# Sinkhorn attention and a residual MLP on one core: part of q loaded in fp32 by SyncE and cast on ScalarE, v sorting and half of a weight permutation on GpSimd

## The chip, the cores and the metric

The kernel runs on one core of a Trainium2 chip. The core has five engines with an instruction stream each: TensorE (PE, matmuls and weight loads), VectorE (DVE), ScalarE (ACT), GpSimd (POOL) and SyncE (SP, which here only starts transfers). Sixteen DMA engines move the data. Transfers started by GpSimd run on the software queue and can change the type on the way; those started by SyncE run on a hardware queue and are loaded in the type that they have. The metric is the device time of one execution in microseconds (us); lower is better.

## What is computed

The attention first normalises a small matrix per batch and head with five Sinkhorn rounds, mixes the blocks of keys and values with it, and attends block by block. Its output goes through a residual MLP over tokens and then over channels.

```
q, k, v: (4, 8, 768, 64)   sort_net: (4, 8, 8, 8)   8 blocks of 96 rows
P = sort_net
5 times:
    P = exp(P - max(P, -1));  P = P / (sum(P, -1) + 1e-9);  P = P / (sum(P, -2) + 1e-9)
k_sorted, v_sorted = einsum('bhij,bhjcd->bhicd', P, blocks of k, of v)
scores = q_block @ k_sorted_block.T / sqrt(64);  attn = softmax(scores)
x = attn @ v_sorted_block, heads side by side                # (4, 768, 512)
a1 = alpha1 * x + beta1
tok = einsum('ts,bsd->btd', w_tok, a1);   u = x + lam * tok   # w_tok: (768, 768)
a2 = alpha2 * u + beta2
ch = max(a2 @ w_ch1, 0) @ w_ch2;  out = u + lam * ch          # w_ch1: (512, 2048), w_ch2: (2048, 512)
```

## The kernel before

The code is one stream of calls in Python; its order is the order on each engine. A small wrapper class (line 55) pins every instruction in program order, which is why nearly all rows of the profile carry line 65; groups are told apart by the names of their tiles. There is no planner: what stands earlier in the text stands earlier in its engine's queue. Two pools of accumulators exist, psA (two wide tiles, `psa`) and psB (four one-bank tiles, `psb`); tiles in SBUF share slots by tag, and a tile that takes a slot over waits until the last reader of the earlier one is done.

The four batches are worked one after another. Batch 0 is special: its operands are loaded and prepared at the start, in an order written out by hand, and this stretch, about the first 36 us, is what the change edits. From then on the matmuls of the MLP of one batch (`h_unit`, `ch_unit`, `ch_pair`) run with the attention of the next put between them, through a table of slots (`put`, `run`).

The stretch in question goes as follows.

- Loads. SP loads P (sort_net), then six small vectors (lines 99 to 108). POOL loads q, k and v of batch 0 with a cast to f16: two transfers of two slabs each for q and k (`load_slabs`), two halves for v (`load_halves`), then w_tok in four pieces (tiles wt), the broadcast vectors alphaB, betaB and lamB, W1p in four parts, W2p in four parts, and later raw v, raw k and qn of batch 1. Between these issues POOL builds the identity (ident), clears padding and copies.
- Sinkhorn rounds (the loop `for it in range(5)`). Each round is one exp on ACT and six small operations on DVE, the last of which writes P again (P16 in the fifth round). After the DVE part of a round come `mask(it)` (small masks msk, mhi, mth, mgap made from the identity) and what the table `beside` lists for it: `q_first(g)` turns slab g of q on PE (q_ps), `q_out(g)` copies it on ACT into qT, `prep_ab2` turns the small vectors, and `warm(n)` fills PE with n matmuls of zeros (warm_ps).
- Mixing. `mix_keys` replicates P16 on PE (repk_ps) and makes the block matrix bigK on DVE (selk, redk, bigK); `mix_values` makes bigV. `k_turn(0, g)` multiplies a slab of k by bigK (k_ps), and `k_copy` brings it to kT on DVE or ACT.
- Values. `v_sort(lo, hi, engine)` copies columns lo to hi of v8 into VD with the last two axes exchanged (vd<-v): in this kernel columns 16 to 32 and 48 to 64 on POOL, 0 to 8 and 8 to 16 on ACT, 32 to 48 on DVE. `v_mix(0, n)` multiplies columns 8n to 8n+8 by bigV (v_ps) into Vs, with one filler matmul in every second call. The gap column of Vs is filled from mgap on DVE.
- Scores and values. `score(0, g, hf, pool)` makes eight matmuls (sc_ps) into a wide tile and one exp of 128 or 96 by 768 on ACT (et). `pv_first(g)` multiplies et by Vs (24 matmuls, x_ps); DVE then takes the reciprocal (rc) and multiplies (x).
- Token weights. `permute(half, engine, lo, hi)` reorders the columns of one half of w_tok (wp<-wt), `wtok(ks)` turns it on PE (wtok_ps) into w_tokT; `row_sum(m)` sums rows of w_tok on ACT (a<-wt, with an accumulator read), `row_sums` turns the three sums into a row (rr_ps, rrow).
- First MLP products. `first_mm(g)` (tok_ps), `first_turn(g)` (turn_ps, with brow = beta1 * lam on POOL), z and tok on ACT, a2T on DVE; then h_ps, the first large product.

Of the kernel before, what the change touches and what calls it, by code (L numbers as in the profile page):

```python
# [16 lines left out]
def kernel(  # L17
# [20 lines left out]
    nc = tc.nc  # L38
# [60 lines left out]
    nc.sync.dma_start(P32[:], sort_net.rearrange("b h i j -> (b h) i j"))  # L99
    ab2 = att.tile([4 * CT, 128], FT, name="ab2", tag="sel", bufs=2)  # L100
# [16 lines left out]
    def load_slabs(dst, src):  # L117
        flat = src[0].rearrange("h s d -> (h s d)").rearrange("(g p f) -> p g f", p=128, f=12 * D)
        for g in range(0, H4, 2):
            pool.dma_start(dst[:, g:g + 2, :], flat[:, g:g + 2, :])  # L120
# [19 lines left out]
    load_slabs(q8, q)  # L140
# [36 lines left out]
    pool.dma_start(alphaB[:], moe_alpha1.partition_broadcast(128))  # L177
    pool.dma_start(betaB[:], moe_beta1.partition_broadcast(128))
    pool.dma_start(lamB[:], moe_lam.partition_broadcast(128))
    v_sort(16, 32, pool.tensor_copy)  # L180
    for g in range(4):
        if g == 1:
            v_sort(48, 64, pool.tensor_copy)
        pool.dma_start(W1p[:, :, g * 512:(g + 1) * 512], w1v[:, :, g * 512:(g + 1) * 512])
    pool.tensor_tensor(brow[0:1, :], bet1[:], lam1[:], ALU.mult)

# [24 lines left out]
    def mask(n):  # L211
# [3 lines left out]
        elif n == 1:  # L215
            dve.tensor_reduce(msk[:], ident16[:].rearrange("p (b j) -> p b j", j=NB), AXX, ALU.add)
            dve.tensor_tensor(mhi[:], msk[:, 0:8], msk[:, 8:16], ALU.add)
            dve.tensor_reduce(mth[:], ident16[:].rearrange("p (th c) -> p th c", th=2), AXX, ALU.add)
        elif n == 2:
# [70 lines left out]
    def q_out(g):  # L290
        for half in range(2):
            q_copy(0, g, qps[g], half, act.copy)

    beside = {
        0: [lambda: q_first(0), lambda: warm(3)],
        1: [lambda: q_first(1), lambda: warm(2), lambda: warm(3)],
        2: [lambda: q_first(2), lambda: warm(3)],
        3: [lambda: q_out(0), lambda: q_first(3)],
# [3 lines left out]
    for it in range(5):  # L302
# [12 lines left out]
        if it < 3:  # L315
# [4 lines left out]

    for g in range(4):
        pool.dma_start(W2p[:, g * 4:(g + 1) * 4, :], w2v[:, g * 4:(g + 1) * 4, :])
# [96 lines left out]
    def score(b, g, hf, ps):  # L419
        ps = ps([128, 2, 512], FT, "sc_ps")  # L420
        n = 128 if b == 0 else BLK
        keys = kT_of[b][:].rearrange("p g i t -> p (g i t)")
        for ii in range(4):
# [3 lines left out]
            for h2 in range(2):  # L427
                r = slice(h2 * 64, h2 * 64 + 64)
                pe.matmul(
                    ps[0:w, h2, ii * BLK:(ii + 1) * BLK], keys[r, lo:lo + w],  # L430
# [4 lines left out]
        act.activation(  # L435
            et[0:n].rearrange("p a i t -> p a (i t)"), ps[0:n, :, 0:4 * BLK], AF.Exp, scale=scale
        )
# [666 lines left out]
```

## Time and profile before

| what | value |
|---|---|
| median of 3 runs | 259.13 us (258.68 to 259.93) |
| profiled execution, its own time | 258.79 us |
| its span, first to last instruction | 257.0 us |
| granted TensorE clock | 1.000 |
| share of the span that the chain of waits gives to PE | 75% |
| the same for DVE, DMA, ACT, issue | 10%, 7%, 4%, 2% |
| repk_ps starts (end of the Sinkhorn rounds) | 11.79 us |
| v of batch 0 complete | 16.38 us |
| first h_ps | 35.88 us |

A row of a timeline gives the start in us, the length in us, the engine, the operation and its tiles as out<-in, how many of them the row holds, and in brackets how long the engine was idle before it and what released it. A row of the chain gives the start, the length and whose work it was; "issue" there is time in which the engine waited for nothing that the profile shows. A row of the windows view gives a stretch, its length, and for PE, weight loads (PEld), DVE, ACT and POOL the busy time and the number of instructions, then the granted clock, the DMA engines' busy share and GB/s. The digits of the slices are tenths of busy time in 40 equal parts of the span, 6.4 us each; the software and the instruction queue are shown with packets, MB and share of the sixteen engines.

### The profile page before, as it was taken

How to read it: one execution, taken by the hardware profiler on the slowest of the kernel's cores; microseconds unless marked ns; L12 is line 12 of the kernel's file. 1: busy time of each engine (PE TensorE's matmuls, PEld its weight loads, DVE VectorE, ACT ScalarE, POOL GpSimd, SP SyncE). 2: the span in 40 equal slices, each digit the busy share in tenths (PEclk: the TensorE clock that was granted, in tenths of full speed). 3: DMA queues.
4: the chain of work that ended last, by engine and by line, in shares of the span. 5: the costliest groups of instructions: out<-in, count | busy, mean ns of one | idle time of the engine just before them, and what ended most of it. 6: DMA issues, size and time to landing. Idle time of an engine off the chain costs nothing.

```text
span 257.0 us, 5959 instructions
## 1 busy us (share of the span) xinstructions
PE 246.4 (96%) x2371; PEld 159.7 (62%) x2371; DVE 176.3 (69%) x467; ACT 155.3 (60%) x282; POOL 44.2 (17%) x67
## 2 busy tenths in 40 slices
PE   7998799999999999999999999999999999999994
PEld 3465565555555545456865787557756875686783
DVE  6796888595539945759896675298887773461873
ACT  3567767485997539787565587877465004847400
POOL 8759302700074000047000000000000000000000
PEclk9999999999999999999999999999999999999999
DMA  5999999998999957999994259810202232111022
GB/s 99 214 203 179 209 205 211 214 151 173 122 209 187 150 128 159 143 136 192 145 143 120 41 135 170 151 20 3 84 0 42 62 101 65 23 40 41 3 82 82
DMA packets 67535, 31.07 MB, mean 121 GB/s; under 512 B 56674, under 2 KB 63218, under 8 KB 67508
## 3 DMA queue, kind: packets, MB, share of 16 engines
q0 software_dynamic: 26352, 15.34, 46.4%
q1 hardware_dynamic: 41060, 15.33, 33.6%
q8 instruction: 18, 0.29, 0.5%
q14 instruction: 9, 0.07, 0.1%
q10 hardware_dynamic: 96, 0.03, 0.1%
HBM read 32.79 MB, written 8.65 MB: 161 GB/s over the span
## 4 chain that ended last, share of the span: by engine, by line
PE 75%; DVE 10%; DMA 7%; ACT 4%; issue 2%; SPq 1%; DVEq 0%; POOLq 0%
PE h_ps L65 27%; PE tok_ps L65 10%; PE px L65 8%; PE pz L65 6%; PE py L65 6%; DVE x L65 5%; PE ch_ps L65 4%; PE x_ps L65 3%; DMA Vs<-vscr 3%; PE warm_ps L65 2%; DMA vscr<-mixed 2%; PE sc_ps L65 2%; DMA q<-in_q_dram 2%; DVE a L65 2%; PE v_ps L65 1%
## 5 line engine op out<-in xcount | busy, mean ns | idle before, releaser
L65 PE MATMUL h_ps<-a2T,W1p 128*128 128x384 bf16 x512 | 93.2, 326 | 0.0
L65 PEld LDWEIGHTS <-W1p 128*128 128x128 bf16 x512 | 47.9, 98 | 31.3 <-issue 0.2
L65 ACT ACTIVATE hTa<-h_ps 128x384 f16<-128x384 f32 x64 | 31.2, 493 | 27.3 <-PE h_ps L65 26.4
L65 ACT ACTIVATE hTb<-h_ps 128x384 f16<-128x384 f32 x64 | 31.2, 490 | 7.6 <-PE h_ps L65 7.6
L65 DVE SCALAR_TENSOR_TENSOR u<-tok_ps,x 128x512 f32<-128x512 f32 x21 | 14.5, 690 | 26.0 <-PE tok_ps L65 26.0
L65 PE MATMUL tok_ps<-a,w_tokT 128*128 128x512 f16 x126 | 30.3, 379 | 0.5 <-DVE a L65 0.5
L65 ACT CAST kT<-kmix_ps 64x512 f16<-64x512 f32 x36 | 25.8, 716 | 4.9 <-PE kmix_ps L65 4.4
L65 ACT ACTIVATE et<-sc_ps 96x768 f16<-96x768 f32 (+1 forms) x32 | 24.8, 808 | 3.7 <-PE sc_ps L65 3.7
L65 ACT CAST u<-u 128x512 f16<-128x512 f32 x21 | 13.0, 618 | 22.9 <-DVE u L65 22.9
L65 PEld LDWEIGHTS <-sums 128*128 128x128 f16 x216 | 21.1, 98 | 3.3 <-issue 0.2
L65 PEld LDWEIGHTS <-hTb 128*128 128x128 f16 x200 | 18.6, 98 | 6.3
L65 PEld LDWEIGHTS <-hTa 128*128 128x128 f16 x192 | 18.3, 98 | 6.4
L65 PEld LDWEIGHTS <-w_tokT 128*128 128x128 f16 x126 | 12.3, 98 | 13.8 <-issue 1.0
L65 DVE TENSOR_TENSOR x<-x_ps,rcb 96x512 f16<-96x512 f32 x24 | 16.5, 687 | 0.8
L65 POOL DMA_DIRECT2D qn<-in_q_dram x18 | 16.0, 913 | 4.3 <-DMA raw<-in_v_dram 4.2
L65 DVE TENSOR_TENSOR sums<-hTa,hTb 128x512 f16<-128x512 f16 (+2 forms) x27 | 8.9, 330 | 10.4 <-ACT hTb L65 10.0
L65 PEld LDWEIGHTS <-et 96*128 96x128 f16 (+4 forms) x288 | 11.8, 100 | 5.3 <-DVE x L65 1.6
L65 PE MATMUL x_ps<-Vs,et 96*128 96x65 f16 (+4 forms) x288 | 13.0, 195 | 1.8 <-DVE x L65 0.9
L65 DVE SCALAR_TENSOR_TENSOR ost<-px,u 128x256 f32<-128x256 f32 x27 | 11.3, 417 | 3.5 <-PE px L65 3.5
L65 PE MATMUL warm_ps<-wz 128*128 128x512 f16 x36 | 11.0, 439 | 1.2 <-DVE wz L65 1.2
L65 PE MATMUL ch_ps<-W2p,hTb 128*128 128x512 f16 x48 | 12.0, 379 | 0.0
L65 ACT CAST mixed<-mix_ps 128x1024 f16<-128x1024 f32 x9 | 9.1, 1012 | 4.7 <-PE mix_ps L65 4.5
(139 smaller groups left out, 352.9 us busy)
## 6 DMA issues: line engine op xcount, KB each, us to landing
out_dram<-ost SPq DMA_DIRECT2D x23, 192.0 KB, 2.7
raw<-in_v_dram POOLq DMA_DIRECT2D x6, 384.0 KB, 6.9
raw<-in_k_dram POOLq DMA_DIRECT2D x6, 384.0 KB, 9.5
qn<-in_q_dram POOLq DMA_DIRECT2D x18, 128.0 KB, 10.5
vscr<-mixed SPq DMA_DIRECT2D x6, 384.0 KB, 5.2
Vs<-vscr SPq DMA_DIRECT2D x3, 768.0 KB
W1p<-in_moe_w_ch_dram POOLq DMA_DIRECT2D x4, 512.0 KB, 11.9
W2p<-in_moe_w_ch_dram POOLq DMA_DIRECT2D x4, 512.0 KB, 17.4
```

Of the source, the lines that this page charges most:

```text
L65: ins = getattr(self.eng, name)(*args, **kwargs)
```

## The change

The first two slabs of q are no longer loaded by POOL with a cast. SP loads them in fp32 into a tile q32, right behind P and ahead of the small vectors, and ACT casts each with two copies, after the exps of the second and the third Sinkhorn round. The q turns and warm-ups in `beside` move accordingly, and the masks are made one per round, with mgap after bigV.

After the rounds, `k_turn(0, 0)` and its copies follow `mix_keys` directly, and `mix_values` takes its accumulator from psA. POOL makes brow, sorts columns 16 to 56 of v and fills the gap column before it issues alphaB, betaB, lamB and W1p; ACT sorts columns 0 to 8 and 56 to 64, DVE 8 to 16. The second half's permute goes from DVE to POOL, between the issues of W1p and W2p. Three of the scores go to two one-bank tiles in psB, with an exp of 384 columns each. The first half's permute is done in one go before the first `pv_first`; the row sums on ACT, `wtok(4)` (DVE to ACT), `pv_first(1)` to `pv_first(3)` and `prep_scales` change places. Nine warm-up matmuls fall away.

```diff
@@ -97,6 +97,11 @@
     dve.memset(wz[:].bitcast(FT), 0.0)
     P32 = const([BH, NB, NB], FT, "P32")
     nc.sync.dma_start(P32[:], sort_net.rearrange("b h i j -> (b h) i j"))
+    q32 = moep.tile([128, 2, 12 * D], FT, name="q32", tag="x128", bufs=1)
+    for g in range(2):
+        nc.sync.dma_start(
+            q32[:, g, :], q[0].rearrange("h s d -> (h s d)").rearrange("(g p f) -> p g f", p=128, f=12 * D)[:, g, :],
+        )
     ab2 = att.tile([4 * CT, 128], FT, name="ab2", tag="sel", bufs=2)
     nc.sync.dma_start(ab2[0:CT, :], moe_alpha2.rearrange("(c p) -> c p", p=128))
     nc.sync.dma_start(ab2[CT:2 * CT, :], moe_beta2.rearrange("(c p) -> c p", p=128))
@@ -114,9 +119,9 @@
     k8 = att.tile([128, H4, 12 * D], F16, name="k8", tag="raw", bufs=2)
     v8 = att.tile([128, HB, D], F16, name="v8", tag="raw", bufs=2)
 
-    def load_slabs(dst, src):
+    def load_slabs(dst, src, lo=0):
         flat = src[0].rearrange("h s d -> (h s d)").rearrange("(g p f) -> p g f", p=128, f=12 * D)
-        for g in range(0, H4, 2):
+        for g in range(lo, H4, 2):
             pool.dma_start(dst[:, g:g + 2, :], flat[:, g:g + 2, :])
 
     def load_halves(dst, src):
@@ -137,7 +142,7 @@
 
     brow = att.tile([128, C], F16, name="brow", tag="uT", bufs=2)
     rrow = att.tile([128, 384], F16, name="rrow", tag="uT", bufs=2)
-    load_slabs(q8, q)
+    load_slabs(q8, q, 2)
     ident16 = const([128, 128], F16, "ident16")
     pool.memset(ident16[:], 0.0)
     pool.affine_select(
@@ -174,16 +179,6 @@
     alphaB = const([128, C], F16, "alphaB")
     betaB = const([128, C], F16, "betaB")
     lamB = att.tile([128, C], FT, name="lamB", tag="kT", bufs=1)
-    pool.dma_start(alphaB[:], moe_alpha1.partition_broadcast(128))
-    pool.dma_start(betaB[:], moe_beta1.partition_broadcast(128))
-    pool.dma_start(lamB[:], moe_lam.partition_broadcast(128))
-    v_sort(16, 32, pool.tensor_copy)
-    for g in range(4):
-        if g == 1:
-            v_sort(48, 64, pool.tensor_copy)
-        pool.dma_start(W1p[:, :, g * 512:(g + 1) * 512], w1v[:, :, g * 512:(g + 1) * 512])
-    pool.tensor_tensor(brow[0:1, :], bet1[:], lam1[:], ALU.mult)
-
     vscr = dram.tile([B, H * NB, BLK, D], F16, name="vscr", tag="vscr")
     raw_of = {}
     qn_of = {}
@@ -214,9 +209,11 @@
             dve.tensor_reduce(mlo[:], ident16[:].rearrange("p (b j) -> p j b", j=NB), AXX, ALU.add)
         elif n == 1:
             dve.tensor_reduce(msk[:], ident16[:].rearrange("p (b j) -> p b j", j=NB), AXX, ALU.add)
+        elif n == 2:
             dve.tensor_tensor(mhi[:], msk[:, 0:8], msk[:, 8:16], ALU.add)
+        elif n == 3:
             dve.tensor_reduce(mth[:], ident16[:].rearrange("p (th c) -> p th c", th=2), AXX, ALU.add)
-        elif n == 2:
+        elif n == 4:
             dve.tensor_reduce(
                 mgap[:], ident16[:].rearrange("p (th t) -> p th t", th=2)[:, :, 0:HB],
                 mybir.AxisListType.XY, ALU.add,
@@ -291,11 +288,15 @@
         for half in range(2):
             q_copy(0, g, qps[g], half, act.copy)
 
+    def q_cast(g):
+        for f in (slice(0, 6 * D), slice(6 * D, 12 * D)):
+            act.copy(q8[:, g, f], q32[:, g, f])
+
     beside = {
-        0: [lambda: q_first(0), lambda: warm(3)],
-        1: [lambda: q_first(1), lambda: warm(2), lambda: warm(3)],
-        2: [lambda: q_first(2), lambda: warm(3)],
-        3: [lambda: q_out(0), lambda: q_first(3)],
+        0: [],
+        1: [lambda: q_cast(0), lambda: q_first(0), lambda: warm(3)],
+        2: [lambda: q_cast(1), lambda: q_first(1), lambda: warm(3), lambda: q_first(2)],
+        3: [lambda: q_out(0), lambda: warm(3), lambda: q_first(3)],
         4: [lambda: q_out(1), lambda: q_out(2), lambda: q_out(3), lambda: prep_ab2(psb), lambda: warm(4)],
     }
     warm(12)
@@ -312,14 +313,11 @@
             (P16 if it == 4 else P32)[:], P32[:],
             csum[:].unsqueeze(1).to_broadcast([BH, NB, NB]), ALU.mult,
         )
-        if it < 3:
+        if it < 4:
             with nc.allow_low_precision(reason="sums of zeros and a one"):
                 mask(it)
         for f in beside[it]:
             f()
-
-    for g in range(4):
-        pool.dma_start(W2p[:, g * 4:(g + 1) * 4, :], w2v[:, g * 4:(g + 1) * 4, :])
 
     bigK = {}
     bigV = {}
@@ -417,7 +415,12 @@
     kT_of = {0: KT0}
 
     def score(b, g, hf, ps):
-        ps = ps([128, 2, 512], FT, "sc_ps")
+        if ps is psb:
+            ps = [ps([128, 4 * BLK], FT, "sc_ps") for _ in range(2)]
+            bank = [t_[:] for t_ in ps]
+        else:
+            ps = [ps([128, 2, 512], FT, "sc_ps")]
+            bank = [ps[0][:, a, :] for a in range(2)]
         n = 128 if b == 0 else BLK
         keys = kT_of[b][:].rearrange("p g i t -> p (g i t)")
         for ii in range(4):
@@ -427,14 +430,20 @@
             for h2 in range(2):
                 r = slice(h2 * 64, h2 * 64 + 64)
                 pe.matmul(
-                    ps[0:w, h2, ii * BLK:(ii + 1) * BLK], keys[r, lo:lo + w],
+                    bank[h2][0:w, ii * BLK:(ii + 1) * BLK], keys[r, lo:lo + w],
                     qT_of[b][r, g, i * BLK:(i + 1) * BLK], start=True, stop=True,
                 )
         tag, bufs = ("ost", 4) if (b, g) == (0, 3) else ("et", 6)
         et = att.tile([128, 2, 4, BLK], F16, name="et", tag=tag, bufs=bufs)
-        act.activation(
-            et[0:n].rearrange("p a i t -> p a (i t)"), ps[0:n, :, 0:4 * BLK], AF.Exp, scale=scale
-        )
+        if len(ps) == 1:
+            act.activation(
+                et[0:n].rearrange("p a i t -> p a (i t)"), ps[0][0:n, :, 0:4 * BLK], AF.Exp, scale=scale
+            )
+        else:
+            for a in range(2):
+                act.activation(
+                    et[0:n, a].rearrange("p i t -> p (i t)"), ps[a][0:n, :], AF.Exp, scale=scale
+                )
         ets[(b, g, hf)] = et
 
     x_of = {}
@@ -891,15 +900,28 @@
         prep_wtok(ks, 0, psb, eng)
 
     mix_keys(0, psb)
-    warm(3)
-    mix_values(0, psb)
-    prep_scales()
-    dve.tensor_copy(Vs[:, :, D:GRP], mgap[:].unsqueeze(2).to_broadcast([128, H * NB, GRP - D]))
     kp0 = k_turn(0, 0, psb)
-    kp1 = k_turn(0, 1, psb)
     k_copy(0, 0, kp0, 0, copy)
     k_copy(0, 0, kp0, 1, act.copy)
-    warm(3)
+    mix_values(0, psa)
+    with nc.allow_low_precision(reason="sums of zeros and a one"):
+        mask(4)
+    pool.tensor_tensor(brow[0:1, :], bet1[:], lam1[:], ALU.mult)
+    v_sort(16, 32, pool.tensor_copy)
+    v_sort(32, 48, pool.tensor_copy)
+    pool.tensor_copy(Vs[:, :, D:GRP], mgap[:].unsqueeze(2).to_broadcast([128, H * NB, GRP - D]))
+    v_sort(48, 56, pool.tensor_copy)
+    pool.dma_start(alphaB[:], moe_alpha1.partition_broadcast(128))
+    pool.dma_start(betaB[:], moe_beta1.partition_broadcast(128))
+    pool.dma_start(lamB[:], moe_lam.partition_broadcast(128))
+    for g in range(4):
+        pool.dma_start(W1p[:, :, g * 512:(g + 1) * 512], w1v[:, :, g * 512:(g + 1) * 512])
+    permute(1, pool.tensor_copy, 0, 6)
+    for g in range(4):
+        pool.dma_start(W2p[:, g * 4:(g + 1) * 4, :], w2v[:, g * 4:(g + 1) * 4, :])
+    warm(1, psa)
+    kp1 = k_turn(0, 1, psb)
+    warm(1)
     kp2 = k_turn(0, 2, psb)
     k_copy(0, 1, kp1, 0, copy)
     k_copy(0, 1, kp1, 1, act.copy)
@@ -907,13 +929,13 @@
     k_copy(0, 2, kp2, 0, copy)
     k_copy(0, 2, kp2, 1, act.copy)
     v_sort(0, 8, act.copy)
-    v_sort(8, 16, act.copy)
+    v_sort(56, 64, act.copy)
     score(0, 0, 0, psa)
     k_copy(0, 3, kp3, 0, copy)
     k_copy(0, 3, kp3, 1, copy)
+    prep_scales()
     score(0, 0, 1, psa)
-    v_sort(32, 48, copy)
-    warm(2, psb)
+    v_sort(8, 16, copy)
     v_mix(0, 0, psb, copy)
     v_mix(0, 1, psb, copy)
     score(0, 1, 0, psa)
@@ -925,31 +947,29 @@
     score(0, 2, 0, psa)
     v_mix(0, 6, psb, copy)
     v_mix(0, 7, psb, act.copy)
-    score(0, 2, 1, psa)
-    row_sum(0)
     permute(0, copy, 0, 3)
+    permute(0, copy, 3, 6)
     moe_start(0)
-    warm(1, psb)
+    score(0, 2, 1, psb)
     pv_first(0)
-    score(0, 3, 0, psa)
     wtok(0, copy)
     wtok(1, act.copy)
     wtok(2, copy)
-    permute(0, copy, 3, 6)
+    row_sum(0)
+    pv_first(1)
+    score(0, 3, 0, psb)
     row_sum(1)
+    pv_first(2)
+    score(0, 3, 1, psb)
     row_sum(2)
-    pv_first(1)
     wtok(3, copy)
-    wtok(4, copy)
+    wtok(4, act.copy)
     wtok(5, copy)
-    permute(1, copy, 0, 6)
-    score(0, 3, 1, psa)
-    pv_first(2)
+    pv_first(3)
     row_sums(psb)
     first_mm(0, psb)
     first_turn(0, psb)
     first_mm(1, psb)
-    pv_first(3)
     first_turn(1, psb)
     first_mm(2, psb)
     scale_affine(alphaB)
```

## The prediction

> **What bounds the kernel now.** I read the page's busy table and its 40 slices first, to find where TensorE is idle; then the chain of waits in order of time, and the waits of PE; then the timelines of DVE, ACT and POOL over the first 36 us, the only stretch that the change touches; last the DMA queues.
>
> ```profile
> PE 246.4 (96%) x2371; PEld 159.7 (62%) x2371; DVE 176.3 (69%) x467; ACT 155.3 (60%) x282; POOL 44.2 (17%) x67
> PE   7998799999999999999999999999999999999994
> DMA  5999999998999957999994259810202232111022
> PEclk9999999999999999999999999999999999999999
> q0 software_dynamic: 26352, 15.34, 46.4%
> q8 instruction: 18, 0.29, 0.5%
> ```
> PE is busy for 246.4 of 257.0 us at full clock. Only slices 1, 4 and 5 and the tail fall under nine tenths, so a gain must come from the first 36 us, where PE is idle for about 5 us, and must then survive to the end. In those slices the DMA engines are nearly full.
>
> ```profile
> 11.86 0.20 PE repk_ps L65 x4
> 13.55 1.04 PE k_ps L65 x48
> 15.34 0.68 PE k_ps L65 x24
> 21.06 1.08 issue
> 22.14 0.47 PE v_ps L65 x19
> 27.68 0.66 issue
> 28.34 0.35 PE x_ps L65 x6
> ```
> This is the chain. It passes the five Sinkhorn rounds (P, q turns and warm-ups up to repk_ps at 11.86), the key mix, the scores and value mix, and holds two pieces of "issue", in which PE waits for no semaphore. They are odd enough to look at: they end at 22.14 and 28.34, and the windows view counts between those two times
>
> ```profile
> 22.14:28.34 6.20, 5.01 (x128) 3.85 (x128) 4.80 (x11) 5.24 (x10) 4.94 (x6) 1.00 1.18 201
> ```
> exactly 128 matmuls and 128 weight loads, 256 PE instructions in 6.20 us. Counting 256 back from 22.14 reaches about 16.15, a stretch of 6.0 us. The DMA view shows packets on the instruction queue (18 in all, 0.29 MB, so 16 KB each) at 19.7 and 25.9 us, each about 2.4 us before a stall ends. I read this as PE waiting for its next 256 instructions, which travel on DMA engines that the software queue keeps full. That fits two stalls only, so it is a reading.
>
> ```profile
> 6.03 0.26 ACT L65 ACTIVATE P<-P 32x64 f32<-32x64 f32 x1 [1.51 <-DVE P L65]
> 8.20 0.26 ACT L65 ACTIVATE P<-P 32x64 f32<-32x64 f32 x1 [1.92 <-DVE P L65]
> 6.23 0.39 DVE L65 TENSOR_TENSOR mhi<-msk 128x8 f16<-128x8 f16 x1
> 6.54 0.27 DVE L65 TENSOR_REDUCE mth<-ident 128x2 f16<-128x128 f16 x1
> 16.43 1.51 POOL L65 COPY vd<-v 128x768 f16<-128x768 f16 x1 [0.57 <-DMA v<-in_v_dram]
> 30.66 1.40 DVE L65 COPY wp<-wt 128x1728 f16<-128x1728 f16 x2
> ```
> Here the reader sees the period of the Sinkhorn rounds (exps at 2.51, 4.27, 6.03, 8.20, 9.96: 1.76 us each, but 2.17 in the third, where two masks sit in front of the row sum), POOL's copy of v waiting for v's landing at 16.38, and DVE's second permute, which holds the reciprocal behind it until 31.97 although its matmuls were done at 30.98.
>
> **The change, part by part.** The sum is made against the profiled execution: 258.79 us, a span of 257.0 and 1.8 around it. It is 0.34 under the median of 259.13, so I add 0.34 at the end.
>
> Masks, one per round: the round of 2.17 falls to 1.76, as msk alone (0.27, from 5.93) ends before the exp does (6.29). mhi (0.39) now stands in the fourth round's gap, in which mgap (0.23) left 0.16 idle: it just fits. Gain 0.41, and P16, done at 11.69, comes at 11.28. PE was itself busy until 11.86 and follows only if its own queue is shorter too, which the casts decide.
>
> q on SyncE: SP's two loads stand behind P's and in front of six small ones, which move back by about 0.8 us (two issues of 0.40). Their readers, the ab_ps turn at 10.7 and brow, have slack: the last landed about 6. POOL issues one DMA fewer (771 ns), so k, v and wt start about 0.8 earlier. The slabs are 768 KB of fp32 for 384 KB cast on the way, but SP's packets of 2048 B took 84 ns and the software queue's of 1536 B 135 ns: 384 packets are 2.0 us of 16 engines, 256 packets were 2.2. So no engine time is saved; what is won is the hole in front, since software packets run dense only from 3.5 us. P landed 1.74 after its issue (0.75 to 2.49). Slab 0, issued at 1.2, would land near 1.2+1.74+1.0 = 3.9, slab 1 a us later at about 5. v then lands 1.0 to 1.2 earlier, near 15.3.
>
> The Trainium skill, page "DMA: Bandwidth & Descriptors", section "Issuing engines are not separate DMA queues", speaks against this step: transfers from SyncE and GpSimd share the same 16 engines, and only sequencer time is saved. By the page alone v would gain only the 0.77 of POOL's issue, and by the rows 1.0 to 1.2, from the idle engines before 3.5.
>
> The casts: four on ACT, nearest row qT at 464 ns for 128x384, about 0.9 a pair. ACT idles 1.50 between exps, so both pairs are covered, if slab 0 lands by 5.1 and slab 1 by 6.9 (exp at 7.79 less 0.9). Later than that, the next exp waits behind the cast on ACT's queue, and DVE's row sum and P16 behind it. PE is tighter still. In its order the second slab's turn is followed by three warm-ups, the third turn, three warm-ups, the fourth turn, the ab_ps turn and four warm-ups: by the chain's pieces 0.49 + 0.75 + 0.49 + 0.75 + 0.49 + 0.16 + 0.97 = 4.1. If the second cast starts as the exp ends, at 6.3, it ends at 7.2 and repk_ps can start at 11.3, tied with P16. So PE loses from a landing of slab 1 after 6.3. Bounds for slab 1: 4.2 (nothing in front) and 8.5, from SP's small loads issued at 2.24 to 2.88 whose packets came at 5.0 to 6.0, 2.8 to 3.1 us later, plus its own transfer behind a full queue. I take 5, by P's row, since it is issued before POOL's data run dense.
>
> Keys, scores, warm-ups: k_turn(0) follows the key mix at once and its copies precede the value masks, so the second pair of k turns moves with P16: 0.4 to 0.6 earlier. The crossing into the next 256 instructions lies in the last k turn in both orders. Gain here -0.5, with bounds 0.3 to 0.6. The count of matmuls falls by nine; warm-ups filled waits, so I price them at nothing, covered by the fetch; without that cover they would be worth at most 9 x 0.25 (three pass in 0.75) = 2.2.
>
> 16 to 28 us: if PE waits for instructions, the 6.0 and 6.2 us stay as they are, whatever the data do: v 1.1 us earlier, a 16-column copy of 1.18 on DVE halved, the gap copy (0.23) off DVE, split exps. All these are priced at 0, covered by the 1.08 + 0.66 of stalls. Should the cover go, the split exps cost most: three of 0.81 become pairs of about 0.45, +0.1 each.
>
> The Trainium skill, page "Runtime: NRT & Kernel Launch", section "Instruction fetch mechanics", says that instructions arrive in blocks of 256 over the sequencer's own queue and that crossing a block is mostly hidden. The size agrees with the 128+128 above; "mostly hidden" does not, with 1.74 us of stalls. By that sentence the stalls would have another cause and the v part would gain up to 1.1 more.
>
> 28 to 36 us: pv_first(1) is now before the crossing, seven matmuls of 0.04 less after it: -0.3. Against it, ACT's three row sums (0.84+0.20 each) now follow the scores; the last may end near 31, so rr_ps at 31.6 instead of 30.9 and PE idle, +0.6. The second permute leaves DVE (1.40), but PE is unbroken there, so 0. I take 0, between the ends -0.3 and +0.6.
>
> POOL: brow (1.26), copies of 1.5, 1.5 and 0.76, and the gap copy (about 0.3) now all stand ahead of alphaB, betaB, lamB (issues 0.60, 0.55, 0.54) and W1p (four of 0.82): W1p issues from about 21 instead of 17.9. The permute on POOL is 2304 elements: 1.9 by DVE's 1.48 times 1513/1180 of the v copies, 4.5 by POOL's 1513 ns for 768. Then W2p goes out from 27 to 29 instead of 24.1, and raw v after it. The queue hides it: lamB, issued at 15.3, landed at 26.33, W1p's last part at 36.47, eleven us and more behind. A hole of up to 1 us may open between wt's end and alphaB. Raw v landed at 50.29 for a use at 51.99, and qn at 60.02 for 60.92, and all starts 0.8 earlier: 0, bounds 0 and +0.5. After 36 us PE is unbroken, and a gain at 36 carries.
>
> Sum: -0.5 (Sinkhorn and keys) + 0 (fetch) + 0 (28 to 36) + 0 (POOL) = 258.3 for this execution, 258.6 against the median.
>
> **The rivals.**
> Stalls go: the earlier start or a less crowded queue lets instructions come in time. Then 1.74 more is won: 258.6 - 1.74 = 256.9. For it: v, the k copies and DVE all have room. Against it: the engines stay full from 3.5 to 50 us.
>
> Slabs late (other side): slab 1 lands behind software packets. From a landing of 6.3 each us costs one, by PE's order; it eats the gain of 0.5 at 6.8, and at 8.5 costs 2.2: 258.6 + 2.2 = 260.8, slower. For it: the 2.8 to 3.1 us of SP's later loads. Against: P's 1.74.
>
> POOL's late issues: if the permute takes 4.5 and a hole of 2 us opens, raw v and qn come 1 us too late: 259.6. Against: the backlog of eleven us.
>
> The change does not do what it says: the scores and row sums on ACT give back all, 259.1.
>
> **How the numbers follow.** Forecast 0.40, stalls go 0.21, slabs late 0.21, POOL late 0.08, all given back 0.10. Half a per cent, 1.3 us, is about what a measurement tells from no change. The forecast's own range is 258.0 to 259.2 and lies within it; faster is the stalls' case and some partial loss of a stall, 0.30; slower is most of slabs late and half of POOL late, with a little unknown, 0.25; same 0.45. The range from 256.7 to 260.5 takes in the first rival and most of the second.
>
> **What would show it.** Exps every 1.76 us with casts between them show the slabs in time; an exp behind a cast that waits for q shows the rival. repk_ps near 11.4 and v landing near 15.3. PE's two issue stalls, 256 instructions apart, at about 21.6 and 27.8: there, the forecast; gone, the first rival. mix_ps or qt_ps waiting for a DMA shows POOL's. I am wrong if the stalls grow, or if row sums on ACT hold rr_ps by more than 0.6.

## The result, and the profile after

The changed kernel takes 261.62 us (median of 5 runs, 260.91 to 261.80) against 259.26 for the kernel before on the same chip: a ratio of 1.008, 95% interval 1.0055 to 1.0105. It is 2.4 us slower; I had forecast 258.6 and a range up to 260.5. The profiled execution is one of 261.65 us with a span of 259.9, 2.9 more than before's 257.0. The ratios here and below leave out executions more than 1.5% above the fastest of the same kernel, four in all.

The page of the changed kernel:

```profile
PE 246.1 (95%) x2362; PEld 159.9 (62%) x2362; DVE 176.6 (68%) x463; ACT 157.5 (61%) x290; POOL 46.3 (18%) x70
PE   8768899999999999989999999999999999999994
PEclk9997999999999999999999999999999999999999
```

PE has as much busy time as before (246.1 against 246.4), though it makes nine warm-ups fewer, and its idle time has grown from 10.6 to 13.8 us. The fourth slice now shows seven tenths of the full clock. The chain of waits says where; the columns are start, length and whose work:

```profile
1.67 5.65 DMA q<-in_q_dram
7.34 0.92 ACT q L65 x2
9.68 1.30 DVE P L65
19.36 1.21 DVE vd L65
26.43 1.36 DVE wp L65 x2
33.46 0.33 PE rr_ps L65 x3
```

The two pieces of "issue" of 1.08 and 0.66 us that the chain held before are gone: the waits of PE hold none for issue, and the two pieces of 0.55 and 0.35 that the chain still has stand in front of DVE's and ACT's work. Other waits took over. Slab 1 of q lands at 7.32 us (1.67 + 5.65); the fourth exp stands behind its cast. A product on DVE lasts 1.30. DVE's copy of v and its permutes are on the path, then ACT's row sums before rr_ps. So repk_ps starts at 12.80 instead of 11.79, the first x_ps at 26.72 instead of 24.52, the first h_ps at 37.64 instead of 35.88.

The timelines of DVE and POOL, side by side, tell more than either does:

```profile
7.50 0.21 DVE L65 TENSOR_TENSOR P<-P,csum 32x64 f32<-32x64 f32 x1
9.68 1.29 DVE L65 TENSOR_TENSOR P<-P,csum 32x64 f32<-32x64 f32 x1
18.59 0.85 DVE L65 TENSOR_TENSOR ab2col<-ab2col 128x4 f32<-128x4 f32 x2
19.36 1.20 DVE L65 COPY vd<-v 128x384 f16<-128x384 f16 x1
```

```profile
9.64 1.25 POOL L65 TENSOR_TENSOR brow<-bet,lam 1x512 f16<-1x512 f32 x1
16.27 2.92 POOL L65 COPY vd<-v 128x768 f16<-128x768 f16 x2 [5.38 <-DMA v<-in_v_dram]
19.38 0.81 POOL L65 COPY vd<-v 128x384 f16<-128x384 f16 x1
20.14 0.62 POOL L65 DMA_DIRECT2D alphaB<-in_moe_alpha_dram  x1
```

Two rows of DVE in the kernel before, for comparison:

```profile
14.42 0.35 DVE L65 TENSOR_TENSOR ab2col<-ab2col 128x4 f32<-128x4 f32 x2
17.45 1.18 DVE L65 COPY vd<-v 128x768 f16<-128x768 f16 x1
```

The product P<-P,csum takes 0.21 us where POOL makes no copy or product; at 7.50 POOL was clearing a tile (a memset, 7.02 to 7.99), and it took 0.21 all the same. In the fourth round it begins as POOL's brow runs, and ends at 10.97, just after brow (10.89). The first of the two ab2col products lasts 0.62 us, until POOL's second copy of v ends (19.19); the second takes 0.19. DVE's copy of v ends 0.4 after POOL's third (20.19). Beside POOL's copies of ebh, from 5.09 to 5.86, a sum (0.25) and a reciprocal (0.19) keep their length, and the product behind them, begun at 5.57, takes 0.37 and ends at 5.94. It is the products with two operands in SBUF, and the f16 copies within SBUF, that wait. The copy of 1.18 in the kernel before may already hold such a wait, as POOL's first copy of v ran until 17.94.

In the changed kernel the second value mix waits for DVE's copy of v, and then the clock goes. In the windows view the columns after the length are PE, PEld, DVE, ACT and POOL, the granted clock, DMA share and GB/s:

```profile
18.00:20.00 2.00, 0.75 (x21) 0.41 (x17) 1.97 (x5) 1.93 (x3) 2.00 (x3) 1.00 1.15 207
20.00:22.00 2.00, 1.39 (x47) 1.04 (x49) 1.79 (x3) 0.63 (x1) 2.00 (x5) 0.97 0.34 60
22.00:24.00 2.00, 2.00 (x51) 1.36 (x49) 0.69 (x1) 1.48 (x3) 2.00 (x3) 0.50 0.65 76
```

PE idles from 18.75 to 20.61, and from about 21.9 to 25.3 its granted clock is a half. In the same rows the DMA engines run dry: 60 GB/s from 20 to 22 us, where the kernel before has 135. POOL issues alphaB at 20.14, 10 us later than before, and nothing else is queued behind w_tok. The last part of W1p lands at 37.52 (36.47 before).

### The profile page after: what moved, and what is told of

The parts are those of the page before. It is cut to its first block, busy times and chain, and to the rows that moved or that the text cites. A ratio compares the mean times of both kernels' runs of the same rounds, so it can differ in the third digit from the quotient of the medians.

```text
span 259.9 us, 5954 instructions
## 1 busy us (share of the span) xinstructions
PE 246.1 (95%) x2362; PEld 159.9 (62%) x2362; DVE 176.6 (68%) x463; ACT 157.5 (61%) x290; POOL 46.3 (18%) x70
## 4 chain that ended last, share of the span: by engine, by line
PE 73%; DVE 10%; DMA 7%; ACT 6%; issue 1%; SPq 1%; DVEq 0%
PE h_ps L65 28%; PE tok_ps L65 10%; PE px L65 8%; PE pz L65 6%; PE py L65 5%; PE ch_ps L65 4%; DMA Vs<-vscr 3%; PE sc_ps L65 2%; DMA q<-in_q_dram 2%; DVE x L65 2%; DMA vscr<-mixed 2%; PE x_ps L65 2%; PE v_ps L65 2%; DVE a L65 1%; DVE ost L65 1%
## 5 line engine op out<-in xcount | busy, mean ns | idle before, releaser
L65 PE MATMUL tok_ps<-a,w_tokT 128*128 128x512 f16 x126 | 30.3, 379 | 0.4 <-DVE a L65 0.4
L65 ACT ACTIVATE et<-sc_ps 96x768 f16<-96x768 f32 (+2 forms) x35 | 25.1, 755 | 4.0 <-PE sc_ps L65 4.0
L65 PE MATMUL ch_ps<-W2p,hTa 128*128 128x512 f16 x48 | 11.8, 379 | 0.0
```

Source lines behind the costliest of these rows:

```text
L65: ins = getattr(self.eng, name)(*args, **kwargs)
```

## Experiments

Ratios are to the kernel before on the same chip, with 95% intervals. A kernel's times behind the median come from several executions, its timeline from one.

### Which part of the Sinkhorn stretch: brow, the slabs, or both undone

brow back behind W1p's issues:

```diff
-    pool.tensor_tensor(brow[0:1, :], ...)          # ahead of the copies of v
     for g in range(4):
         pool.dma_start(W1p[...], w1v[...])
+    pool.tensor_tensor(brow[0:1, :], bet1[:], lam1[:], ALU.mult)
     permute(1, pool.tensor_copy, 0, 6)
```

> The changed kernel with one edit: GpSimd's product brow goes back behind the four issues of W1p, out of the Sinkhorn rounds. Port theory: in the changed kernel DVE's product P<-P,csum of the fourth round, 0.21 us elsewhere, lasts 1.29 us (9.68 to 10.97) because GpSimd's brow runs from 9.64 to 10.89 and the two engines cannot both read SBUF operands; here it is 0.21 again, the fifth exp comes about 1.07 earlier, P16 at about 11.65 instead of 12.73. TensorE's own queue then sets repk_ps, at about 12.5 instead of 12.80, so the time falls by only 0.3 to 0.5, to about 261.2. Rival, something else on DVE (its instructions coming late): the 1.29 us stay, and so does the time, 261.6.

Measured 262.87 us, 1.0147 (1.0108 to 1.0186): slower, not faster. The profiled execution is one of the two slowest of six (264.57). In it the product of the fourth round took 0.21 again, as expected, but slab 1 landed at 8.32, a microsecond later still, and hid what brow gave; and POOL's permute, pushed back by brow, now met DVE's permutes, for which wtok_ps waited 2.0 us. A miss.

q by GpSimd again, casts gone:

```diff
-    q32 = ...; nc.sync.dma_start(q32[:, g, :], ...)
-    load_slabs(q8, q, 2)
+    load_slabs(q8, q)
-        1: [lambda: q_cast(0), lambda: q_first(0), lambda: warm(3)],
+        1: [lambda: q_first(0), lambda: warm(3)],        # and the same for q_cast(1)
```

> The changed kernel with q loaded by GpSimd with a cast, as before, and no casts on ScalarE; all else as changed. Late-slab theory: the fourth exp no longer waits behind the cast of slab 1 (which landed at 7.32 us) and the rounds are 1.76 us each up to the fourth; brow, one transfer issue later at about 10.4 us, then holds a product of the fifth round, so P16 comes at about 11.8 and repk_ps at about 11.9 instead of 12.80: 0.9 less, 260.7. Port theory alone: P16 stays late by one blocked product, 0.4 less at most. Rival, the slabs do not matter since v and the values set the time: 261.6 unchanged.

Measured 261.42, 1.0098 (1.0078 to 1.0117). repk_ps came at 12.10, 0.7 earlier, but the second value mix began at 20.66 as in the changed kernel (20.61): it now waited 2.2 us for DVE's copy of v instead of 1.9. The gain ended there.

Both edits together:

> Both edits: q by GpSimd and brow behind W1p's issues; what is left of the change is the order on TensorE, DVE and GpSimd from 12 us on, and the masks. If the two things are the whole loss of the Sinkhorn stretch, P16 comes at about 11.3 and repk_ps at about 11.35, 1.45 earlier than in the changed kernel, and the time is 261.6 - 1.45 = 260.2. If the loss is mostly behind 16 us (v's copy on DVE, the halved clock from 22 to 25 us, the row sums), the gain is swallowed there by waits and the time stays over 261.

Measured 263.01, 1.0162 (1.0142 to 1.0182). repk_ps starts at 11.83. PE then waits 2.1 us for DVE's copy of v and 2.3 for DVE's permutes (four copies of 4.15 us that took 1.34 before; brow and POOL's permute ran beside them), and the clock is halved twice. Being early in front did no good, since the next wait is on POOL, and what was taken out of one collision ran into another.

The port alone, on the kernel before: brow moved forward, ahead of alphaB.

```diff
+    pool.tensor_tensor(brow[0:1, :], bet1[:], lam1[:], ALU.mult)
     pool.dma_start(alphaB[:], ...)
```

> The kernel before with one edit: brow goes on GpSimd right behind the issues of w_tok, ahead of alphaB's, so that it runs from about 10.4 to 11.65 us, inside the fifth round. Port theory: DVE's product that starts while brow runs (P<-P,rsum at 10.7, 0.21 us before) lasts until brow ends, about 11.7, and P16 comes at 12.6 instead of 11.69: about 0.9 later up to k_ps, and the time is 0.5 to 0.9 longer, 259.8 to 260.2. Without a shared port: unchanged, 259.3.

The timelines of this kernel, first DVE, then POOL:

```profile
10.48 0.19 DVE L65 RECIPROCAL rsum<-rsum 32x8 f32<-32x8 f32 x1
10.71 1.03 DVE L65 TENSOR_TENSOR P<-P,rsum 32x64 f32<-32x64 f32 x1
```

```profile
10.40 1.26 POOL L65 TENSOR_TENSOR brow<-bet,lam 1x512 f16<-1x512 f32 x1
```

Beside brow the reciprocal keeps its 0.19 us, and the product takes 1.03 instead of 0.21. That DVE's product waits for POOL's is shown. repk_ps came 0.76 later (12.55). Yet the time was 259.27, 1.0018 (1.0004 to 1.0032), about 0.5 us: the two issue stalls shrank from 1.08 and 0.66 to 0.33 and 0.39, and h_ps came only 0.24 later. The stalls absorb delays, as the forecast had it, up to their size.

The rule is in the Trainium skill, page "SBUF — State Buffer", section "Who interferes with whom": a DVE instruction with two inputs in SBUF contends with a GpSimd instruction that reads SBUF, and one that uses both ports (f16 copies can) with any; whoever starts first holds the shared ports for its whole length. The rows agree in both kinds, and the last of all runs below has a copy held by a copy that began before it (1.07 us instead of 0.51). The other order occurs too: in the first run of this section DVE's copy of v and POOL's began together at 20.31, DVE's kept 0.51 us, and POOL's took 1.22 instead of 0.81. My prediction did not use this rule, and it speaks against the change in three places.

### Which part behind 16 us: v's copy, the permute, the clock

Columns 8 to 16 on ACT, 56 to 64 on DVE later, the two products back behind the value mask:

```diff
-    v_sort(56, 64, act.copy)
+    v_sort(8, 16, act.copy)
-    prep_scales()          # behind the key copies
-    v_sort(8, 16, copy)
+    v_sort(56, 64, copy)   # behind score(0, 1, 1)
     mix_values(0, psa)
+    prep_scales()
```

> The changed kernel with v's columns 8 to 16 on ScalarE again, as before, columns 56 to 64 on VectorE behind the fourth value mix, and the two small scale products (ab2col) back behind the value mask. Theory: in the changed kernel the second value mix waits 1.86 us for DVE (18.75 to 20.61), because DVE's ab2col products (0.85 for two that took 0.35) and its copy of v (1.20) stand behind GpSimd's copies of v; TensorE's idling then halves its granted clock from about 21.9 to 25.3 us. Here the second value mix waits at most 0.3, the clock stays at 1.00, the first x_ps comes about 2.5 earlier than 26.72, and the time falls by 1.5 to 2.5, to 259.1 to 260.1. Rival, the row sums on ScalarE and DVE's permutes set the end of the stretch: rr_ps stays at 33.5 and the time at 261.

Measured 261.50, 1.0086 (1.0059 to 1.0113), from 259.6 to 262.9. The wait was gone and h_ps came at 36.33, but then x_ps waited 1.1 us for Vs and qt_ps 0.2 for qn, which the kernel before did for 0.2 and not at all. The clock, expected to stay at 1.00, was halved from 15.2 to about 22 us.

The second permute on DVE again:

```diff
-    permute(1, pool.tensor_copy, 0, 6)
     wtok(5, copy)
+    permute(1, copy, 0, 6)
```

> The changed kernel with the second half's permute on VectorE again, behind its last w_tokT copy of the stretch. Port theory: GpSimd's permute (24.77 to 27.07) holds DVE's first-half permutes, four copies of 2.09 us from 26.43 that took 1.34 in the kernel before; here they take 1.34 and the first wtok_ps comes 0.6 earlier; 0.4 to 0.7 less time, 261.0. Against it: 1.40 us more work on DVE beside x. Rival, the permute on GpSimd helps as meant: the time rises to 262 or more.

Measured 261.72, 1.0097 (1.0069 to 1.0124): no change. In its profile qt_ps waited 1.3 us for qn.

Six filler matmuls in the second value mix:

```diff
-        fill(..., 1 - n % 2)
+        fill(..., 6 if (b, n) == (0, 1) else 1 - n % 2)
```

> The changed kernel with six filler matmuls of zeros in the second value mix, into its own accumulator, where TensorE waited 1.86 us for DVE; nothing else. Clock theory: the wait itself stays (v_ps again at about 20.6), but TensorE counts as busy, the granted clock stays at 1.00 from 21 to 26 us, that stretch is 1.5 us shorter, and the time falls by 1.0 to 1.5, to 260.4. Rival, the low clock costs nothing since the stretch waits for others: unchanged at 261.6.

Measured 261.42, 1.0081 (1.0049 to 1.0112). The profiled execution is inconclusive: in it the clock was halved from 17.1 us on already, before the fillers, which themselves ran at half rate (six in 2.74 us). But two of the seven executions had a mean clock of 1.00 and took 261.66 and 263.38, so a full clock alone does not bring the time back.

All four undone: the diffs above for q, the columns and the permute, and brow behind W2p's issues:

```diff
-    pool.tensor_tensor(brow[0:1, :], ...)      # ahead of the copies of v
         pool.dma_start(W2p[...], w2v[...])
+    pool.tensor_tensor(brow[0:1, :], bet1[:], lam1[:], ALU.mult)
```

> All of it undone at once: q by GpSimd, brow behind W2p's issues, columns 8 to 16 on ScalarE, the second permute on VectorE. What is left of the change: one mask per round, the order of the key turns and of row sums and scores, v's other columns on GpSimd ahead of W1p, split exps, fewer warm-ups. If the four are the whole loss, no wait on DVE or ACT over 0.6 us is left before 28 us, the clock is 1.00, h_ps starts at 35.9 or earlier and the time is 258.0 to 259.3, the kernel before or better. If the order left over costs too (row sums last, W1p late), it is 260 or more.

Measured 261.73, 1.0093 (1.0075 to 1.0112). The first of its views is the timeline of PE, the second has rows of the waits of PE from 40 to 120 us (us in total, times, longest):

```profile
21.61 0.37 PE L65 MATMUL v_ps<-bigV,vd 64*64 64x64 f16 x11 [0.41 <-issue]
27.81 0.93 PE L65 MATMUL x_ps<-Vs,et 128*128 128x65 f16 x21 [0.99 <-issue]
35.45 0.74 PE L65 MATMUL h_ps<-a2T,W1p 128*128 128x384 bf16 x3
```

```profile
PE qt_ps L65 <- DMA qn<-in_q_dram: 1.7, 2, 1.4
PE x_ps L65 <- DMA Vs<-vscr: 0.8, 1, 0.8
PE mix_ps L65 <- DMA raw<-in_v_dram: 0.4, 1, 0.4
```

Now the stretch is as I had forecast it: repk_ps at 11.54, the stalls back, ending 6.20 us apart as before, h_ps 0.43 ahead of the kernel before. And the kernel is as slow as the changed one, since PE waits 2.9 us for transfers, of which the kernel before waited 0.2. The loss has a second source, which shows only when PE is early.

### The transfers

The kernel with four things undone, and alphaB, betaB, lamB and W1p issued early again:

```diff
+    pool.dma_start(alphaB[:], ...)      # and betaB, lamB, behind w_tok
     v_sort(16, 32, pool.tensor_copy)
+    pool.dma_start(W1p[:, :, 0 * 512:1 * 512], ...)
     v_sort(32, 48, pool.tensor_copy)
+    pool.dma_start(W1p[:, :, 1 * 512:2 * 512], ...)
     pool.tensor_copy(Vs[:, :, D:GRP], ...)
     v_sort(48, 56, pool.tensor_copy)
-    pool.dma_start(alphaB[:], ...)      # and betaB, lamB, W1p's first two parts
```

> The kernel of the run before with all four things undone (261.7), and one edit more: alphaB, betaB, lamB go out behind w_tok again and the four parts of W1p between the copies of v, as before the change. Transfer theory: there h_ps started at 35.45 us, 0.4 ahead of the kernel before, but TensorE then waited 0.4 for raw v, 1.7 for qn and 0.8 for Vs, since the software queue had run dry from 20 to 24 us and everything behind came 1 to 3 us later; with the queue fed these waits fall to 0.3 in all and the time is 258.8 to 259.2, the kernel before or a little under. Rival, the order of row sums, scores and warm-ups costs by itself: 260.5 or more.

Measured 259.64, 0.9999 (0.9975 to 1.0022): the kernel before, no faster. PE no longer waits for raw v or qn, but still 1.0 us for Vs. Together with the run before it this prices the late issues at 0.9%, where nothing else is late. The key and score order, the masks, the split exps and the row sums of the change, which are all still in it, together come out even to within about 0.25%.

The changed kernel with the early issues alone, by the same diff:

> The changed kernel with only this edit: alphaB, betaB, lamB and W1p issued early as before the change. If late transfers alone set the time, it falls to 259.5. If the late stretch on the engines (slab 1, brow, v's copies, halved clock, row sums) costs as much beside them, h_ps still starts near 37.6 and the time stays at 260.7 to 261.5: two losses side by side, each enough.

Measured 261.37, 1.0068 (1.0046 to 1.0090); h_ps at 37.87, no wait for transfers behind it. Two losses side by side, each enough.

The kernel before with the issues late alone:

```diff
+    v_sort(16, 32, pool.tensor_copy)
+    v_sort(48, 64, pool.tensor_copy)
     pool.dma_start(alphaB[:], ...)      # then betaB, lamB, W1p in four parts
-    v_sort(16, 32, ...); v_sort(48, 64, ...)   # between the parts of W1p
```

> The kernel before with one edit: GpSimd makes both its copies of v before it issues alphaB, betaB, lamB and W1p. Transfer theory: alphaB goes out at about 19.5 us instead of 10.4, the DMA engines thin out from 20 to 23 us, W1p, raw v and qn land about 1 us later, the slack of 1.5 for raw v and 0.9 for qn is used up and qt_ps waits 0.3 to 1.5: 259.6 to 261. Rival, my forecast's reading that the backlog hides it: unchanged, 259.3.

Measured 261.43, 1.0080 (1.0057 to 1.0103). The size was as expected and the way was not: h_ps came at 38.15 and nothing waited for qn. brow, pushed back behind W1p, ran from 24.76 to 26.11 into DVE's first permute (1.55 us instead of 0.66), the second stall grew to 1.36, and the clock was halved from 30.3 to about 33.3 us. Three of the six executions had a mean clock of 0.999 or more and took 261.3 to 261.5 all the same. So the run was made once more with brow out of the way:

```diff
-    pool.tensor_tensor(brow[0:1, :], bet1[:], lam1[:], ALU.mult)   # behind W1p's issues
+    pool.tensor_tensor(brow[0:1, :], bet1[:], lam1[:], ALU.mult)   # behind W2p's issues
```

> The kernel before with the late loads (both copies of v on GpSimd ahead of alphaB, betaB, lamB and W1p), and brow moved behind W2p's issues, away from DVE's first permute, which it held for 0.9 us in the run with the late loads alone (261.4, 0.8% slower; h_ps at 38.15 us). If the loss there was DVE held by brow, with longer instruction stalls and the halved clock behind it, most of it goes: 259.6 to 260. If the late transfers carry it, TensorE is early again (h_ps near 36) and waits for qn and Vs instead, as in the kernel with four things undone: 261 to 261.7.

Its waits of PE from 40 us on:

```profile
PE qt_ps L65 <- DMA qn<-in_q_dram: 1.6, 2, 1.4
PE x_ps L65 <- DMA Vs<-vscr: 0.7, 1, 0.7
```

Measured 261.16, 1.0066 (1.0039 to 1.0093). h_ps starts at 35.61, ahead of the kernel before, the clock is 1.00, and qt_ps waits 1.6 us: W1p's last part landed at 37.61 and the last qn at 62.84 instead of 60.02. Here the late transfers carry the loss alone.

The q part alone, on the kernel before:

```diff
+    q32 = ...; nc.sync.dma_start(q32[:, g, :], ...)     # two slabs, behind P
-    load_slabs(q8, q)
+    load_slabs(q8, q, 2)
+    q_cast, and the table of the change for q turns and warm-ups
```

> The kernel before with only the q part: slabs 0 and 1 in fp32 by SyncE, cast on ScalarE, with the table of q turns and warm-ups of the change; masks as before. In profiles of kernels with this part slab 1 landed at 5.7, 7.3, 8.3 and 8.3 us, a different time in each execution. Theory: an early landing leaves the time at 259.2, a late one moves the fourth exp and all behind it by up to 1.6 us, of which the instruction stalls (1.74 us) take some; median 259.3 to 260.3 and a spread over 1 us. Rival: no cost beyond the spread of the kernel before.

Measured 259.34, 0.9994 (0.9979 to 1.0009). Slab 1 landed at 7.35 and repk_ps came at 12.47, 0.7 late; the stalls were 0.75 and 0.36, and h_ps came at 35.93, as before. On its own the part is free in the median; one execution of the twelve, outside the ratio, took 265.63.

### One part at a time, put back

Undoing had hidden one loss behind another, so the parts were put back singly into the kernel with all five undone (0.9999). brow first:

```diff
+    pool.tensor_tensor(brow[0:1, :], ...)     # ahead of alphaB
-    pool.tensor_tensor(brow[0:1, :], ...)     # behind W2p
```

> Base of this and the next three: the kernel with all five things undone (early loads), which equals the kernel before. One part of the change put back: brow on GpSimd right behind w_tok's issues, inside the Sinkhorn rounds. Port theory: one product on DVE waits for it, P16 comes 0.9 to 1.1 later; the instruction stalls behind (0.82 and 0.99 in the base) absorb most, as they did with the kernel before: 0.2 to 0.5 slower, 259.9. If brow alone carries the loss of the change: 1.5 to 2.4 slower.

Measured 259.95, 1.0031 (1.0015 to 1.0047). The blocked product took 0.68 us, as it began when brow was half over. The two executions with a mean clock of 1.00 took 259.16 and 259.45; in the profiled one the clock was halved for some 3 us from about 20.5 us on, so part of the price may be the clock's.

The permute:

```diff
+    permute(1, pool.tensor_copy, 0, 6)     # ahead of W2p
-    permute(1, copy, 0, 6)                 # behind wtok(5)
```

> One part put back: the second half's permute on GpSimd between W1p and W2p. Port theory: it runs about 23 to 25.5 us, where DVE makes its first-half permutes, which must wait up to 1.5 us; first wtok_ps and x_ps come later, TensorE idles and may drop to half clock: 0.5 to 2 slower. Rival: DVE gains 1.40 us further on and it comes out even, 259.6.

Measured 259.40, 1.0004 (0.9993 to 1.0015): free. DVE's four first-half permutes took 2.85 us instead of 1.34 and wtok_ps waited 1.0, but the instruction stall behind was shorter by half (0.45 instead of 0.99).

The columns of v, with the place of the two products:

```diff
-    prep_scales()            # behind mix_values
-    v_sort(8, 16, act.copy)
+    v_sort(56, 64, act.copy)
+    prep_scales()            # behind the key copies
+    v_sort(8, 16, copy)
-    v_sort(56, 64, copy)
```

> One part put back: v's columns 8 to 16 on DVE behind the ab2col products, 56 to 64 on ScalarE. Port theory: the products and the copy on DVE wait for GpSimd's copies of v, the second value mix waits 1.6 to 2.3 us for DVE, and TensorE's clock is halved for 3 us in the 24 that follow; even with the instruction stalls absorbing up to 1.7 it is 1 to 2.5 slower, 260.6 to 262. If TensorE's idling is absorbed altogether: 259.6.

The timeline of DVE, and below it the windows with the columns as above:

```profile
17.41 3.28 DVE L65 TENSOR_TENSOR ab2col<-ab2col 128x4 f32<-128x4 f32 x2
20.61 0.51 DVE L65 COPY vd<-v 128x384 f16<-128x384 f16 x1
```

```profile
18.00:20.00 2.00, 0.00 (x0) 0.00 (x0) 1.97 (x2) 1.60 (x3) 2.00 (x3) 0.63 1.17 214
20.00:22.00 2.00, 0.83 (x24) 0.77 (x24) 1.87 (x4) 0.00 (x0) 2.00 (x5) 0.50 1.18 161
```

Measured 262.08, 1.0105 (1.0086 to 1.0123): more than the whole loss. Two products of four numbers a partition take 3.28 us, and DVE's copy of v stands behind them. The first lasts 0.69, until POOL's first copy of v has ended (18.07). The second runs from 18.13 to 20.69, over all of POOL's second copy (18.74 to 20.23) and for 0.6 us before it and 0.5 after it; what held it in these two pieces is not shown. PE waits 3.2 us and then runs at half clock. h_ps comes at 38.75.

The q part:

```diff
+    q32 = ...; nc.sync.dma_start(q32[:, g, :], ...); load_slabs(q8, q, 2); q_cast
-    load_slabs(q8, q)
```

> One part put back: slabs 0 and 1 of q in fp32 by SyncE with casts on ScalarE. As with the kernel before and this part alone (ratio 0.9994): 0 to 0.5 slower, with a wider spread. If it matters only with the change's order: 1 or more slower.

Measured 260.19, 1.0032 (1.0004 to 1.0060), from 258.6 to 263.2: a little slower, and wide. Of the twelve, 262.72 and 263.19 are outside the ratio. The profiled execution is the one of 262.72: slab 1 landed at 8.95, past my bound of 8.5, and repk_ps came at 14.07.

Last, the run with v's copy put back, with only the two products moved ahead of the key copies:

```diff
     mix_values(0, psa)
+    prep_scales()
-    prep_scales()          # behind the key copies, ahead of v_sort(8, 16, copy)
```

> The run before with v's copy on DVE put back (262.1, 1.05% slower), and in it only the two ab2col products (0.35 us together when nothing holds them) moved back ahead of the key copies. Port theory: there the products waited behind two of GpSimd's copies of v in turn (17.41 to 20.69), and DVE's copy of v behind them; without the products DVE's copy waits for one of GpSimd's only, ends near 18.5 instead of 21.1, the second value mix waits 0.6 instead of 3.2, the clock stays at 1.00 and the time is 259.4 to 260.2. Rival, DVE's copy of v is at fault by itself: 261.5 or more.

The copy in the timeline of DVE, and what PE waited for from 10 to 40 us:

```profile
17.26 1.07 DVE L65 COPY vd<-v 128x384 f16<-128x384 f16 x1
```

```profile
PE x_ps L65 <- issue: 1.0, 1, 1.0
PE v_ps L65 <- DVE vd L65: 0.5, 1, 0.5
```

Measured 259.36, 1.0021 (1.0002 to 1.0040); the second value mix waits 0.5 us, the clock stays at 1.00, h_ps comes at 35.42. Of 1.05% the place of two products of 0.35 us made 0.84.

## Why the prediction was wrong

The forecast was that the instruction stalls pace PE and a gain of 0.5 us from the rounds carries to the end. It fell by two prices of 0 that each cost the whole loss, and by one collision that I had not priced. No run undid these two alone and left brow, slabs and permute as changed; that the two are enough is put together from single runs.

- Masks, +0.41 forecast: right. In the kernel with four things undone the exps stand at 2.30, 4.06, 5.83, 7.59 and 9.35, 1.76 us apart all through, and repk_ps comes at 11.54, h_ps 0.43 earlier than before. The row of 0.39 for mhi was misread: it had stood beside POOL's copies of ebh, and took 0.14 when moved.
- "The queue hides it", with "0, bounds 0 and +0.5" for POOL's late issues: this step failed. I took the time from an issue to its landing, eleven us, as a backlog that a later issue can eat into. But those eleven us are the queue's content at the time of issue; ten us later it had drained. Engines ran at 60 GB/s from 20 to 22 us. The measured price is 0.66% on the kernel before (with brow out of the way) and 0.9% between the kernels with four and with five things undone, about 1.7 to 2.4 us. Its rival was there, with a hole of 2 us and 259.6: the hole was right, the price was half, since in the kernel with late issues and brow away qn came 2.8 us late where raw v came 1.1 late.
- "All these are priced at 0, covered by the 1.08 + 0.66 of stalls" (16 to 28 us), DVE's halved copy of v among them: failed. Halving DVE's copy was no gain once it stood behind two products and all of them beside POOL's longer work. Alone, that is 1.05%, of which 0.84 is the place of the two products, which has no term in the sum at all. The stalls did cover delays, 0.76 us of repk_ps down to 0.24 at h_ps, but a wait of 1.9 to 3.2 us is more than the cover of 1.74, and the clock was halved on top, at a price that no run shows by itself.
- brow in the rounds: not priced at all. It cost 1.08 us on DVE's chain (1.29 instead of 0.21), 0.2 to 0.3% of the time alone.
- Slab 1: forecast 5 us, landed at 7.32, and in other executions up to 8.95, past the far bound of 8.5. The rival on this took place as a mechanism: the fourth exp waited. In the median it costs 0 to 0.3%, as the stalls take it up. v landed at 16.14, 0.24 earlier and not 1.1.
- The stalls: gone in the changed kernel, which I had set as the sign of the first rival. But PE was late for other reasons there, and nothing was won; in the kernel with four things undone they are back, 1.40 us in all.
- Row sums: rr_ps waits 0.5 us for ACT in nearly all kernels with the change's order, just inside the forecast's bound of 0.6, and the kernel with five things undone is none the slower.
- Nine warm-ups fewer, priced at nothing: open. The kernels without them kept the full clock in some executions and lost it in others; no run put them back alone.
- After 36 us, "a gain at 36 carries": not borne out. In the last run above h_ps came 0.46 earlier than before, but PE then waited 0.9 us for Vs, and the time is level.

Late PE and late transfers do not add. From the first h_ps to the end there are 220.6 to 221.8 us and the waits for transfers in each of these profiles: 37.64 to 259.9 with 0.9 of waits in the changed kernel, 35.61 to 259.4 with 2.3 in the one with late issues and brow away. If PE is late, the transfers are in time. This is why undoing any one thing gave nothing. Why the changed kernel waits 0.9 us for Vs instead of 0.2 stays open: that wait was 0.2 to 1.0 in kernels level with the one before.

No version beat the kernel before. Those level with it had the first h_ps between 35.4 and 36.1 us against 35.88.

## What to carry over

Before moving work to GpSimd, lay its timeline over VectorE's: in these runs a product with two SBUF inputs, or an f16 copy, that VectorE began beside a running GpSimd copy or product lasted at least until that one ended, however small it was, and what stood behind it in order waited too. A queue in front of a transfer hides a later issue only for as long as it holds data at the new time of issue. When undoing parts one at a time gives nothing, undo all of them and put them back singly: two losses side by side hide each other.

## What I had not expected

Two products on 128 x 4 numbers, 0.35 us in all, moved a few calls down the text, were worth 0.84% (3.28 us in the timeline).

The granted clock can halve without a long gap. In the changed kernel with columns 8 to 16 of v back on ACT it fell to 0.50 at 15.2 us, after a stretch from 12 us on in which no idle gap was longer than 0.5 us and PE was busy for 1.12 of the first 2 us. In the kernel before, with more warm-ups, PE was busy for 1.61 of the same 2 us and the clock stayed at 1.00. But the share alone does not decide it: the kernel with five things undone had 1.12 there too and kept 1.00, so what sets the fall stays open. The Trainium skill, page "TensorE: Matmul & The Clock Gate", section "What's actually happening", has a free-running window of about 3.4 us over which activity is judged. The falls to exactly 0.50, and their absence at the same share, agree with it; no run here shows the window itself.

The load of slab 1 by SyncE, issued at 1.67 us, landed at 5.7, 6.1, 6.1, 7.3, 7.35, 8.3, 8.3 and 8.95 us in eight profiled executions, while slab 0, issued 0.45 earlier, landed at 4.0 to 4.4 in all of them.
